# Attention and mixture of experts in one kernel: another hand-written order of transposes, routing steps and gating chain

## The chip, the cores and the metric

The kernel runs on one core of a Trainium2 chip. The metric is the device time of one execution in microseconds; before the change its median of three runs is 856.85 us (855.57 to 857.64). In the profile PE is the matrix engine (PEld its weight loads), DVE the vector engine, ACT the scalar engine, POOL GpSimd and SP the queue that issues most DMAs. The five engines run their own instruction queues, each in its order, and wait for each other by semaphores.

## The reference

Causal attention with a bias made from a cumulated sum, for 8 x 8 heads of 576 positions of 64 values, then a mixture of eight experts of which every token uses one:

```
cum = cumsum(max(s, 0))
scores = q @ k.T / 8 + min(-(cum[i] - cum[j]), 0)      # masked above the diagonal
attn_out = softmax(scores) @ v                         # per batch and head
x = attn_out with heads joined: (8 * 576, 512)
logits = x @ w_gate;  e = argmax(logits);  g = softmax(logits)[e]
out[token] = g * (max(x @ w1[e], 0) @ w2[e])           # e of that token
```

All in float32.

## The kernel before

The attention part works on 32 pairs of heads; four pairs are one batch element of 576 tokens. The rows of a pair are cut into four groups of 128 queries (0 to 3, with 128, 256, 384 and 512 keys, since later keys are masked) and a mixed group 4 that holds the last 64 rows of both heads (576 keys). The loop in `Attention.loop` goes over 32 x 5 units; `n` is the unit, `j = n % 5` its place in the pair, and `ORD` gives the groups in the order 3, 0, 2, 4, 1.

For each group of a pair there are these steps. `scores` (line 217) makes the score tile `s` in PSUM with four matmul terms per head: bias, and three products of high and low parts of q and k. `rowmax` (L257, DVE) reads `s`, adds the mask, and writes `z` and its row minimum `m`. `expo` (L271, ACT) writes the exponentials to `E`. `trans` turns `E` by half transposes on PE (L275) into a PSUM tile `t`, which DVE or ACT copies into `aT` (L297, L298: groups 0, 1, 4 on DVE, 2 and 3 on ACT). `av` (L308) multiplies a whole pair's `aT` with v, one pair later, and DVE copies the result into `xb` (L297). The next pair's q and k are split into high and low parts meanwhile, on ACT (L191, L197) and POOL (L194, L201).

PSUM tiles come from two pools of two buffers: `s` for scores and, while attention runs, for the routing steps; `t` for transposes and `av`. A score tile waits until DVE has read the tile two before it. `z` has four buffers.

After each fourth pair a batch element is routed, in eight steps that `begin` and `end` issue between the attention units, two a pair, both at j = 4: one ahead of the scores of group 1 and one behind the transposes there. Step 0 is the gating product (L351, with `w_gate`, copied to `LT` by ACT), step 1 turns `LT` (L275) and multiplies by the softmax denominators (`part`, L365). A chain of small DVE operations and one exponential follows (L373 to L394: logits, their maximum, the one-hot expert `oh`, the gate value). Step 2 ranks tokens within their expert by small matmuls (L401 to L404) and DVE operations (L410 to L416) and yields row numbers `dsi`. Steps 3 to 7 turn and scale 128 tokens each (L426, into `xr`). Once `dsi` is there, POOL scatters the rows to the experts' lists by indirect DMAs (L437), one per unit. The seventh batch element (b = 6) takes steps faster, since the first expert's load needs it; the eighth is routed after the loop, beside the first expert's work.

The order on PE, DVE and ACT is the order in which this code is written. The order on POOL and SP is made by a scheduler. `transposes` lag three units behind their scores (`LAG`), `expo` one unit; the list `STEPS` gives the order of the routing steps. `constants` (L817 to L849) fills small tables for routing with DVE and POOL.

## Time and profile before

| | |
|---|---|
| median of three runs | 856.85 us (855.57 to 857.64) |
| the profiled execution | 850.7 us, span 849.0 us, mean granted clock 0.980 |
| busy over the span | PE 784.9, PEld 624.1, DVE 483.7, ACT 426.2, POOL 209.3 us |
| attention | from the first scores at 9.28 us to the last value run at 379.8 us |

The profiled execution is 6.2 us below the median of the runs; differences worked out inside it are carried over to the median. In a row of the order of time stand the start in us, the duration, the engine, the line, the operation, output and inputs by the program's names, the shape, the count, and in brackets the idle time of the engine just before and what ended it. A matmul row with x2 or x12 joins as many instructions.

### The profile page before, as it was taken

The page shows a single profiled execution, that of the slowest core. Times are in us where ns is not written, and L with a number is a line of the kernel's source. Part 1 is how long each engine was busy: PE and PEld are TensorE (multiplying, and loading weights), DVE is VectorE, ACT ScalarE, POOL GpSimd, SP SyncE. Part 2 cuts the span into 40 slices and gives each one's busy share as a digit, 9 for nine tenths or more (in the row PEclk, how much of TensorE's full clock was granted, in tenths as well). Part 3 has the DMA queues.
Part 4 walks back from the last instruction along what each step waited for, and adds up shares of the span by engine and source line. Part 5 has one row for each costly group of instructions (what it writes and reads, how often), then busy time and mean ns, then how long its engine had stood idle before and what let it go on. Part 6 is the DMA issues. An engine that isn't in the chain of part 4 may idle for free.

```text
span 849.0 us, 17331 instructions
## 1 busy us (share of the span) xinstructions
PE 784.9 (92%) x6708; PEld 624.1 (74%) x6708; DVE 483.7 (57%) x1264; ACT 426.2 (50%) x1006; POOL 209.3 (25%) x309
## 2 busy tenths in 40 slices
PE   6899898998998999799989999999999999899994
PEld 4677766676767776566878878888888888788883
DVE  6777878787878777768516445353362263542511
ACT  5787777777777777663315233332251251422401
POOL 5333535363545444502010100001001001001010
PEclk8899999999999999899999999999999999999997
DMA  6373424243333332155955354351161062531110
GB/s 218 118 228 105 139 88 144 89 138 95 109 100 106 107 125 80 39 169 201 283 170 178 124 162 163 128 183 38 44 227 68 18 225 87 188 125 33 50 50 15
DMA packets 43901, 105.21 MB, mean 124 GB/s; under 512 B 3983, under 2 KB 3983, under 8 KB 43792
## 3 DMA queue, kind: packets, MB, share of 16 engines
q1 hardware_dynamic: 35408, 80.13, 29.6%
q0 software_dynamic: 5936, 18.92, 6.2%
q10 hardware_dynamic: 2448, 4.74, 1.6%
q8 instruction: 66, 1.08, 0.5%
q14 instruction: 43, 0.35, 0.1%
HBM read 75.91 MB, written 28.12 MB: 123 GB/s over the span
## 4 chain that ended last, share of the span: by engine, by line
issue 40%; PE 31%; DVE 11%; DMA 7%; ACT 3%; another core or an unknown queue 3%; POOL 3%; POOLq 1%; SPq 0%; DVEq 0%; ACTq 0%
PE s L217 12%; PE t L308 8%; DMA out_dram<-y,xr 6%; DVE z L257 5%; PE t L275 4%; PE ph L651 3%; PE py L673 3%; POOL out_dram L680 2%; ACT E L271 2%; PE s L351 1%; DMA raw<-in_w_dram 1%; DVE aT L297 1%; ACT q L191 1%; ACT kh L197 1%
## 5 line engine op out<-in xcount | busy, mean ns | idle before, releaser
L673 PE MATMUL py<-w2t,hT 128*128 128x512 f32 x768 | 181.6, 392 | 0.0
L651 PE MATMUL ph<-xT,w1t 128*128 128x512 f32 x768 | 178.4, 391 | 3.3 <-issue 2.4
L271 ACT ACTIVATE E<-z,m 128x512 f32<-128x512 f32 (+4 forms) x288 | 165.2, 577 | 22.4 <-DVE m L257 22.0
L257 DVE CUSTOM_DVE_ANT_0 z<-s,mask 128x512 f32<-128x512 f32 (+4 forms) x288 | 139.3, 517 | 53.9 <-PE s L217 18.8
L651 PEld LDWEIGHTS ph<-xT,w1t 128*128 128x128 f32 x768 | 143.3, 188 | 34.9 <-issue 4.9
L673 PEld LDWEIGHTS py<-w2t,hT 128*128 128x128 f32 x768 | 142.5, 188 | 28.9
L680 POOL DMA_INDIRECT out_dram<-y,xr x39 | 38.0, 975 | 397.3 <-DVE y L679 355.8
L217 PE MATMUL s<-cu,pick 64*128 64x512 f32 (+4 forms) x320 | 76.7, 397 | 26.9 <-DVE m L257 19.2
L308 PE MATMUL t<-aT,v 128*64 128x64 f32 (+4 forms) x1152 | 96.8, 322 | 3.2 <-DVE aT L297 3.2
L275 PEld LDWEIGHTS t<-ident,E 64*128 64x128 f32 x1600 | 72.6, 141 | 33.6 <-ACT E L271 21.9
L653 ACT ACTIVATE hT<-ph 128x512 fp32r<-128x512 f32 x64 | 38.3, 598 | 108.6 <-PE ph L651 108.1
L679 DVE TENSOR_SCALAR y<-py,xr 128x512 f32<-128x512 f32 x35 | 26.3, 751 | 114.1 <-PE py L673 114.1
L298 ACT COPY aT<-t 128x1024 f32<-128x1024 f32 x64 | 57.9, 905 | 62.5 <-PE t L275 62.5
L654 DVE SCALAR_TENSOR_TENSOR hT<-ph,hT 128x512 fp32r<-128x512 f32 x64 | 44.3, 692 | 73.1 <-ACT hT L653 72.9
L217 PE MATMUL s<-kh,q 64*128 64x384 f32 (+3 forms) x512 | 84.2, 327 | 0.0
L275 PE MATMUL t<-ident,E 64*128 64x64 f32 x1600 | 81.4, 228 | 2.9 <-DVE xb L297 1.7
L308 PEld LDWEIGHTS t<-aT,v 128*64 128x64 f32 x1152 | 51.9, 139 | 25.2 <-issue 15.5
L217 PEld LDWEIGHTS s<-cu,pick 64*128 64x128 f32 (+1 forms) x320 | 39.4, 194 | 40.8 <-DVE m L257 14.7
L568 ACT ACTIVATE xT<-t 128x512 fp32r<-128x512 f32 x32 | 18.4, 597 | 89.5 <-PE t L624 89.5
L297 DVE COPY aT<-t 128x256 f32<-128x256 f32 (+2 forms) x96 | 61.6, 642 | 0.7 <-PE t L275 0.6
L194 POOL TENSOR_TENSOR q<-qk,q 128x576 fp32r<-128x576 f32 x31 | 44.4, 1431 | 60.9 <-ACT q L191 60.8
L271 ACT ACTIVATION_READ_ACCUMULATOR E<-z,m 128x1 f32 x288 | 54.5, 189 | 0.0
(155 smaller groups left out, 1027.7 us busy)
## 6 DMA issues: line engine op xcount, KB each, us to landing
raw<-in_w_dram SPq DMA_DIRECT2D x32, 1024.0 KB, 5.5
qk<-in_qkv_dram SPq DMA_DIRECT2D x32, 576.0 KB, 3.8
v<-in_qkv_dram SPq DMA_DIRECT2D x32, 320.0 KB, 3.6
xr<-xs SPq DMA_DIRECT2D x8, 1028.0 KB, 5.6
xs<-blank ACTq DMA_DIRECT2D x9, 514.0 KB, 6.1
xs<-blank SPq DMA_DIRECT2D x8, 514.0 KB, 8.5
xr<-xs SPq DMA_DIRECT2D x8, 514.0 KB, 6.4
xs<-xr,dsi POOLq DMA_INDIRECT x40, 3.4
```

The lines of the kernel that those rows point to most:

```text
L194: e.tensor_tensor(out=d["q"][:, 1], in0=q, in1=d["q"][:, 0].bitcast(F32), op=ALU.subtract)
L217: self.nc.tensor.matmul(out, terms[n][0], terms[n][1], start=n == 0, stop=n == len(terms) - 1, skip_group_check=True)
L257: ins = nc.vector.tensor_tensor_reduce(out=cut(z[:, :w]), in0=x, in1=mask, scale=-0.125, scalar=3.0e38, op0=ALU.add, op1=ALU.min, accum_out=m,
L271: nc.scalar.activation(out, z[:, :w], AF.Exp, bias=m, scale=-1.0, accum_out=total)
L275: self.nc.tensor.transpose(out, src[r], self.K["ident"][r, r])
L297: return self.nc.vector.tensor_copy(o, i)
L298: return self.nc.scalar.copy(o, i)
L308: nc.tensor.matmul(ps[64 * h : 64 * h + 64, bank, lo - 512 * bank : hi - 512 * bank], v[:, kt, h], self.aT[p % 2][:, kt, h, lo:hi], start= ...
L651: nc.tensor.matmul(ps, w[:, a, d, c], x[:, b, d], start=n == 0, stop=n == 11)
L654: nc.vector.scalar_tensor_tensor(out=h[:, 1, f], in0=ps, scalar=0.0, in1=h[:, 0, f].bitcast(F32), op0=ALU.max, op1=ALU.subtract)
L673: self.nc.tensor.matmul(ps, hT[:, a, f, c], w[:, b, f % 4], start=f == 0 and i == 0, stop=f == 7 and i == 2)
L680: disjoint(self.tc, "out", self.nc.gpsimd.indirect_dma_start(out=self.out, out_offset=IndirectOffsetOnAxis(ap=row[:, DM + 1 : DM + 2].bitc ...
```

## The change

It reorders what the loop issues and alters no arithmetic. The table `TURNS` replaces the fixed lag: at j = 1 the transposes of groups 4 and 1 of the pair before, at j = 3 those of group 3, at j = 4 those of groups 0 and 2 of the same pair. `EXPS` does the same for the exponentials. The steps of a batch element come as 3, 0, 1, 4, 5, 6, 2, 7, so that the token step 3 stands first behind the value run and the gating product second; batch 6 takes 3, 0, 1, 2, 4, 5, 6, 7 with one extra step a pair at j = 1 (before: at j = 1 and j = 2). The gating chain yields once more, behind its exponential, and its halves run at j = 3 of two successive pairs (both at once for batch 6). `constants` is a generator now, and its three pieces run in the first three units instead of all in the seventh.

```
--- before.py
+++ after.py
@@ -33,7 +33,8 @@
 ORD = (3, 0, 2, 4, 1)
 MIX = 4
 NG = len(ORD)
-LAG = 3
+TURNS = {1: (4, 1), 3: (3,), 4: (0, 2)}
+EXPS = {1: (3,), 2: (0,), 3: (2, 4), 4: (1,)}
 FILL0, FSTEP, FILL_END = 9, 2, 28
 RUNP = NPAIR
 WARM = 24
@@ -41,7 +42,8 @@
 SPLIT_AT = (0, 1, 0, 1, 3, 2)
 EVAC = {0: "V", 1: "V", 2: "A", 3: "A", 4: "V"}
 AV_AT = 3
-STEPS = (0, 3, 1, 4, 2, 5, 6, 7)
+STEPS = (3, 0, 1, 4, 5, 6, 2, 7)
+HASTE = (3, 0, 1, 2, 4, 5, 6, 7)
 W_STEP = 2
 THIN_AT = (2, 2)
 X0 = (1, 2, 1)
@@ -315,7 +317,7 @@
         if x == 3:
             r = dict(b=b, xb=xb)
             self.scale(r)
-            self.rq += [(r, i) for i in (range(self.NROUTE) if b >= RUNP // 4 - 2 else STEPS)]
+            self.rq += [(r, i) for i in (STEPS, HASTE, range(self.NROUTE))[max(0, b - RUNP // 4 + 3)]]
         self.copy("V", xb[:, x, :S], ps.rearrange("p a c -> p (a c)")[:, :S])
         self.st.pop(p)
 
@@ -381,6 +383,7 @@
             nc.vector.tensor_reduce(out=mx, in_=L, op=ALU.max, axis=AX.X)
             nc.vector.tensor_tensor(out=dd, in0=L, in1=mx.unsqueeze(2).broadcast_to([P, 5, 8]), op=ALU.subtract)
             nc.scalar.activation(ex, dd, AF.Exp)
+            yield
             nc.vector.scalar_tensor_tensor(
                 out=sc, in0=dd, scalar=0.0, in1=K["w8"].unsqueeze(1).broadcast_to([P, 5, 8]),
                 op0=ALU.is_ge, op1=ALU.mult,
@@ -453,16 +456,19 @@
         self.load(1)
         self.load_v(1)
         self.rq, self.sq, self.chain = [], [], None
-        soon = lambda: self.rq and self.rq[0][0]["b"] == RUNP // 4 - 2
+        hasty = lambda: self.rq and self.rq[0][0]["b"] == RUNP // 4 - 2
+        todo = constants(self.nc, self.const, self.K, self.wg)
         for n in range(nu + NG - 1):
             j = n % NG
+            now = n < nu
             first = None
-            if n < nu:
+            due = self.sq.pop(0) if self.sq and n >= FILL_END else None
+            if now:
                 p, g = steps[n]
                 if j == 0 and p + 2 < RUNP:
                     self.load(p + 2)
                     self.load_v(p + 2)
-                if n >= FILL0 and n < FILL_END and (n - FILL0) % FSTEP == 0 and self.nfill <= E:
+                if n >= FILL0 and (n - FILL0) % FSTEP == 0 and self.nfill <= E:
                     self.fill(self.nfill)
                     self.nfill += 1
                 if j == 4:
@@ -475,29 +481,32 @@
                 self.rowmax(p, g)
                 if first:
                     self.end(first)
-                if n == 6:
-                    constants(self.nc, self.const, self.K, self.wg)
-            due = self.sq.pop(0) if self.sq and n >= FILL_END else None
-            if j != 4 and 0 < n <= nu:
-                self.expo(*steps[n - 1])
+                next(todo, None)
+            if now:
+                for x in EXPS.get(j, ()):
+                    self.expo(p, x)
             if j == AV_AT:
-                if n < nu:
-                    self.expo(p, g)
                 if self.chain:
                     next(self.chain, None)
-                    self.chain = None
+                    if self.chained == RUNP // 4 - 2:
+                        next(self.chain, None)
                 if n >= NG:
                     self.av(n // NG - 1)
-            if 0 <= n - LAG < nu:
-                self.trans(*steps[n - LAG])
-            if n < nu and (j == 4 or j in (1, 2) and soon()):
+            for x, g2 in enumerate(TURNS.get(j, ())):
+                q = n // NG - (j == 1)
+                if 0 <= q < RUNP:
+                    self.trans(q, g2)
+                if now and j == 4 and x == 0:
+                    self.end(self.begin())
+            if now and j == 1 and hasty():
                 self.end(self.begin())
-            if n < nu and p + 1 < RUNP:
+            if now and p + 1 < RUNP:
                 for x in range(6):
                     if SPLIT_AT[x] == j:
                         self.split(p + 1, x)
             if due:
                 self.scatter(*due)
+        assert self.nfill > E
         assert all(r["b"] == RUNP // 4 - 1 for r, *x in self.rq + self.sq)
         self.open = False
 
@@ -505,9 +514,6 @@
         if not self.rq:
             return None
         r, x = self.rq.pop(0)
-        if x == 2 and self.chain:
-            next(self.chain, None)
-            self.chain = None
         todo = self.route(r, x)
         next(todo)
         return r, x, todo
@@ -517,7 +523,7 @@
             r, x, todo = step
             next(todo, None)
             if x == 1:
-                self.chain = todo
+                self.chain, self.chained = todo, r["b"]
             r.setdefault("ready", [])
             if x > 2:
                 r["ready"].append((r, x - 3))
@@ -528,9 +534,8 @@
     def finish(self):
         while self.rq:
             self.end(self.begin())
-            if self.chain:
-                next(self.chain, None)
-                self.chain = None
+            while self.chain:
+                self.chain = self.chain if next(self.chain, 0) is None else None
         while self.sq:
             self.scatter(*self.sq.pop(0))
 
@@ -823,23 +828,25 @@
     ramp = cp.tile([P, 8], I32, name="ramp")
     K["w8"] = cp.tile([P, 8], F32, name="w8")
     nc.gpsimd.iota(ramp, pattern=[[-1, 8]], base=8, channel_multiplier=0)
-    nc.vector.tensor_copy(K["w8"], ramp)
     ramp2 = cp.tile([P, 8], I32, name="ramp2")
     K["base0"] = cp.tile([P, 8], F32, name="base0")
     K["base"] = cp.tile([P, 8], F32, name="base")
     K["first"] = cp.tile([P, 8], F32, name="first")
     nc.vector.memset(K["first"], float(P * NSTAT))
     nc.gpsimd.iota(ramp2, pattern=[[STRIDE, 8]], base=0, channel_multiplier=0)
-    nc.vector.tensor_copy(K["base0"], ramp2)
-    nc.vector.tensor_copy(K["base"], ramp2)
     one = cp.tile([P, P], F32, name="one")
     nc.vector.memset(one, 1.0)
     low = cp.tile([P, P], F32, name="low")
     nc.gpsimd.affine_select(
         out=low, in_=one, pattern=[[1, P]], compare_op=ALU.is_gt, fill=0.0, base=0, channel_multiplier=-1
     )
+    yield
+    nc.vector.tensor_copy(K["w8"], ramp)
+    nc.vector.tensor_copy(K["base0"], ramp2)
+    nc.vector.tensor_copy(K["base"], ramp2)
     K["both"] = cp.tile([P, HP], F32, name="both")
     nc.vector.tensor_tensor(out=K["both"], in0=K["ident"][:, :HP], in1=K["ident"][:, HP:], op=ALU.add)
+    yield
     K["before"] = cp.tile([P, P], BF16, name="before")
     K["ones"] = cp.tile([P, P], BF16, name="ones")
     K["ones64"] = cp.tile([P, P], BF16, name="ones64")
```

The line numbers below are those of each program: what is line 217, 275, 297, 351, 373 before, is 219, 277, 299, 353, 375 after. `E_107`, `E_104`, `E_106`, `E_108` and `E_105` are the exponentials of groups 3, 0, 2, 4 and 1.

First place: PE at the end of a pair that has the gating product, from the transposes of group 3 behind the value run to the first scores of the next pair. Before:

```order
L275 MATMUL t<-ident,E_107 128x64 x16
L351 MATMUL s<-xb_197,wg 32x288 x8
L217 MATMUL s<-cu,pick 128x256 x2
L217 MATMUL s<-kh,q 128x256 x2
L217 MATMUL s<-kl,q 128x256 x2
L217 MATMUL s<-kh,q 128x256 x2
L275 MATMUL t<-ident,E_104 128x64 x4
L275 MATMUL s<-ident,xb_197 128x64 x8
L217 MATMUL s<-cu,pick 128x512 x2
```

And after:

```order
L277 MATMUL t<-ident,E_107 128x64 x16
L277 MATMUL s<-ident,xb_197 128x64 x8
L219 MATMUL s<-cu,pick 128x256 x2
L219 MATMUL s<-kh,q 128x256 x2
L219 MATMUL s<-kl,q 128x256 x2
L219 MATMUL s<-kh,q 128x256 x2
L277 MATMUL t<-ident,E_104 128x64 x4
L353 MATMUL s<-xb_197,wg 32x288 x8
L277 MATMUL t<-ident,E_106 128x64 x12
L219 MATMUL s<-cu,pick 128x512 x2
```

The gating product (`xb,wg`) and the eight token transposes have changed places, and the twelve transposes of group 2 now stand ahead of the 512-wide scores instead of behind them. In the other pairs the two routing steps are others, and the transposes of group 2 stand in the same new place.

Second place: PE in the middle of a pair, from the last scores of group 0 to the first of group 4. Before:

```order
L217 MATMUL s<-kh,q 128x128 x2
L275 MATMUL t<-ident,E_108 128x64 x10
L217 MATMUL s<-cu,pick 128x384 x2
L217 MATMUL s<-kh,q 128x384 x2
L217 MATMUL s<-kl,q 128x384 x2
L217 MATMUL s<-kh,q 128x384 x2
L275 MATMUL t<-ident,E_105 128x64 x8
L217 MATMUL s<-cu,pick 128x288
```

And after:

```order
L219 MATMUL s<-kh,q 128x128 x2
L277 MATMUL t<-ident,E_108 128x64 x10
L277 MATMUL t<-ident,E_105 128x64 x8
L219 MATMUL s<-cu,pick 128x384 x2
L219 MATMUL s<-kh,q 128x384 x2
L219 MATMUL s<-kl,q 128x384 x2
L219 MATMUL s<-kh,q 128x384 x2
L219 MATMUL s<-cu,pick 128x288
```

The eight transposes of group 1 have moved ahead of the 384-wide scores; behind these the scores of group 4 follow at once.

Third place: DVE in the third pair of a batch element's routing, from the start of the gating chain to the copy of the value product. Before, the whole chain:

```order
L373 TENSOR_TENSOR both<-part 128x160
L375 TENSOR_REDUCE L<-both 128x40
L381 TENSOR_REDUCE mx<-L 128x5
L382 TENSOR_TENSOR dd<-L,mx 128x40
L384 SCALAR_TENSOR_TENSOR sc<-dd,w_410 128x40
L389 TENSOR_REDUCE m_1455<-sc 128x5
L390 TENSOR_TENSOR oh<-sc,m_1455 128x40
L392 TENSOR_REDUCE sm<-ex 128x5
L393 TENSOR_SCALAR sm<-sm 128x5
L394 RECIPROCAL xr<-sm 128x5
L297 COPY xb_204<-t 128x576
```

After, in the third pair:

```order
L375 TENSOR_TENSOR both<-part 128x160
L377 TENSOR_REDUCE L<-both 128x40
L383 TENSOR_REDUCE mx<-L 128x5
L384 TENSOR_TENSOR dd<-L,mx 128x40
L299 COPY xb_204<-t 128x576
```

and in the fourth pair, where nothing of the chain stood before:

```order
L387 SCALAR_TENSOR_TENSOR sc<-dd,w_247 128x40
L392 TENSOR_REDUCE m_1652<-sc 128x5
L393 TENSOR_TENSOR oh<-sc,m_1652 128x40
L395 TENSOR_REDUCE sm<-ex 128x5
L396 TENSOR_SCALAR sm<-sm 128x5
L397 RECIPROCAL xr<-sm 128x5
L299 COPY xb_204<-t 128x576
```

The chain is cut behind the difference `dd`; its second half stands one pair later, and the ranking step, which needs `oh`, with it.

More of the change, by code (lines that the diff above doesn't have):

```diff
@@ L455, in loop @@
         self.rq, self.sq, self.chain = [], [], None
-        soon = lambda: self.rq and self.rq[0][0]["b"] == RUNP // 4 - 2
+        hasty = lambda: self.rq and self.rq[0][0]["b"] == RUNP // 4 - 2
+        todo = constants(self.nc, self.const, self.K, self.wg)
         for n in range(nu + NG - 1):
             j = n % NG
+            now = n < nu
             first = None
-            if n < nu:
+            due = self.sq.pop(0) if self.sq and n >= FILL_END else None
+            if now:
                 p, g = steps[n]
@@ L477, in loop @@
                     self.end(first)
-                if n == 6:
-                    constants(self.nc, self.const, self.K, self.wg)
-            due = self.sq.pop(0) if self.sq and n >= FILL_END else None
-            if j != 4 and 0 < n <= nu:
-                self.expo(*steps[n - 1])
+                next(todo, None)
+            if now:
+                for x in EXPS.get(j, ()):
+                    self.expo(p, x)
             if j == AV_AT:
-                if n < nu:
-                    self.expo(p, g)
                 if self.chain:
                     next(self.chain, None)
-                    self.chain = None
+                    if self.chained == RUNP // 4 - 2:
+                        next(self.chain, None)
                 if n >= NG:
                     self.av(n // NG - 1)
-            if 0 <= n - LAG < nu:
-                self.trans(*steps[n - LAG])
-            if n < nu and (j == 4 or j in (1, 2) and soon()):
+            for x, g2 in enumerate(TURNS.get(j, ())):
+                q = n // NG - (j == 1)
+                if 0 <= q < RUNP:
+                    self.trans(q, g2)
+                if now and j == 4 and x == 0:
+                    self.end(self.begin())
+            if now and j == 1 and hasty():
                 self.end(self.begin())
-            if n < nu and p + 1 < RUNP:
+            if now and p + 1 < RUNP:
                 for x in range(6):
@@ L507, in begin @@
         r, x = self.rq.pop(0)
-        if x == 2 and self.chain:
-            next(self.chain, None)
-            self.chain = None
         todo = self.route(r, x)
@@ L840, in constants @@
     )
+    yield
+    nc.vector.tensor_copy(K["w8"], ramp)
+    nc.vector.tensor_copy(K["base0"], ramp2)
+    nc.vector.tensor_copy(K["base"], ramp2)
     K["both"] = cp.tile([P, HP], F32, name="both")
     nc.vector.tensor_tensor(out=K["both"], in0=K["ident"][:, :HP], in1=K["ident"][:, HP:], op=ALU.add)
+    yield
     K["before"] = cp.tile([P, P], BF16, name="before")
```

22 lines of the change are left out of this document (11 added, 11 removed).

## The prediction

> **What bounds the kernel now.** I read the table of stages first, then the order of time on PE inside one attention pair, then who ends PE's waits there. Names: S3, S0, S2, S4, S1 are the score matmuls of a pair in the order of issue; M, X and T with the same number are that group's row minimum on DVE, exponentials on ACT and transposes on PE; xb is the copy of the value product; A and B are the two routing steps of a pair.
>
> The page's group of first score matmuls and the stage of one full turn of four pairs (columns: stretch, its length, busy time of PE, PE's weight loads, DVE, ACT, POOL, granted clock, DMA):
>
> ```profile
> L217 PE MATMUL s<-cu,pick 64*128 64x512 f32 (+4 forms) x320 | 76.7, 397 | 26.9 <-DVE m L257 19.2
> 112.67:157.41 44.74, 40.79 (x584) 31.32 (x582) 34.57 (x117) 33.88 (x90) 21.04 (x30) 1.00 0.35 111
> ```
>
> Four pairs take 44.74 us, PE is busy for 40.79 of them, DVE for 34.57, ACT for 33.88. PE is nearest to its bound but idle for 3.95 us a turn, and most of the idle time before scores ends with a row minimum. The clock is 1.00. Where the idle time lies, one pair with A and B both token steps (PE):
>
> ```profile
> 133.54 0.49 PE L217 MATMUL s<-cu,pick 64*128 64x512 f32 x2 [0.47 <-DVE base L416]
> ...
> 134.55 0.56 PE L275 MATMUL t<-ident,E 64*128 64x64 f32 x12
> 134.89 0.33 PE L217 MATMUL s<-cu,pick 64*128 64x128 f32 x2
> ...
> 135.37 0.52 PE L275 MATMUL t<-ident,E 64*128 64x64 f32 x10
> 136.14 0.44 PE L217 MATMUL s<-cu,pick 64*128 64x384 f32 x2 [0.25 <-DVE m L257]
> ...
> 136.95 0.41 PE L275 MATMUL t<-ident,E 64*128 64x64 f32 x8
> 137.29 0.40 PE L217 MATMUL s<-cu,pick 128*128 128x288 f32 x1
> ...
> 138.54 3.06 PE L308 MATMUL t<-aT,v 128*64 128x64 f32 x36
> 141.54 0.71 PE L275 MATMUL t<-ident,E 64*128 64x64 f32 x16
> ...
> 143.29 0.46 PE L275 MATMUL s<-ident,xb 64*128 64x64 f32 x8
> 144.10 0.50 PE L217 MATMUL s<-cu,pick 64*128 64x512 f32 x2 [0.36 <-DVE m L257]
> ```
>
> and DVE in the same pair (M3's second half, xb, the token scaling of A, M1's second half):
>
> ```profile
> 135.39 0.69 DVE L257 CUSTOM_DVE_ANT_0 z<-s,mask 128x512 f32<-128x512 f32 x1
> ...
> 141.66 0.76 DVE L297 COPY xb<-t 128x576 f32<-128x576 f32 x1 [1.27 <-PE t L308]
> ...
> 142.54 0.69 DVE L426 TENSOR_TENSOR xr<-s,rr 128x512 f32<-128x512 f32 x1
> ...
> 143.53 0.42 DVE L257 CUSTOM_DVE_ANT_0 z<-s,mask 128x256 f32<-128x256 f32 x1
> ```
>
> The pair has two fixed distances. S2 needs the bank of S3: M3 ends at 136.08, S2 starts at 136.14, 2.60 us after S3. The next S3 needs the bank of S1: M1 ends at 143.95, S3 starts at 144.10, 2.56 us after T3. Between them PE never waits: S2 0.81, T1 0.34, S4 1.25, the value run 3.00. So pair = 2.60 + 5.40 + 2.56 = 10.56. T2 stands in the first distance, T1 in the middle, and at both ends PE idles.
>
> **The change, part by part.** *The two transposes.* T1 moves ahead of S2 into the first distance, T2 out of it and ahead of the next S3. The first distance then holds T1's 0.34 in place of T2's 0.34 (134.55 to 134.89) and stays 2.60. The middle loses T1: 5.06. T2 lands in the 0.81 us from B's start to S3, of which B's eight transposes need 0.34, like T1's eight, and T2 0.34; the second distance stays 2.56, set by xb, the token scaling and M1 on DVE, which all hang on the value run. Each routed pair loses 0.34; T1's and T2's copies keep their engines, and ACT's queue keeps its order. Pairs with no routing step have no such idle time: T2 adds there what T1 saves, nothing. Bounds: 0 (T2 held by T3's copy on ACT) to 0.34 + 0.36, the whole wait of S3. I take 0.34.
>
> *The gating product second.* With it first, and waiting for xb, the pair of the product goes so; the last row is the same product later, unhindered:
>
> ```profile
> 152.10 0.71 PE L275 MATMUL t<-ident,E 64*128 64x64 f32 x16
> 152.75 1.56 PE L351 MATMUL s<-xb,wg 128*32 128x288 f32 x16
> ...
> 156.06 0.50 PE L217 MATMUL s<-cu,pick 64*128 64x512 f32 x2 [0.55 <-DVE m L257]
> ...
> 385.88 1.18 PE L351 MATMUL t<-xb,wg 128*32 128x288 f32 x16
> ```
>
> T3 to S3 is 3.96, since S1 and M1 stand behind the 1.5 us of product. After the change the token step is first; its last transposes wait for xb (ready 0.88 after T3), so its scaling on DVE ends near 1.9 after T3, where above it ended at 1.69. Then B, the product, 1.1 (385.88 to its end at 387.06, less the drain), then T2 0.34: 3.4. M1 is done by 2.8 and no longer counts. Saved 0.55 a turn; bounds 0 and 3.96 - 2.56 = 1.4.
>
> *The gating chain in halves.* Before, all of it stands between M4 and xb in one pair; rows of PE's T3, the chain's first and xb behind its last, and the ranking's first and last on DVE:
>
> ```profile
> 129.97 0.71 PE L275 MATMUL t<-ident,E 64*128 64x64 f32 x16
> ```
> ```profile
> 128.73 0.32 DVE L373 TENSOR_TENSOR both<-part 128x160 f32<-128x160 f32 x1
> ...
> 131.15 0.72 DVE L297 COPY xb<-t 128x576 f32<-128x576 f32 x1
> ...
> 132.47 0.20 DVE L410 TENSOR_TENSOR t<-s,base 128x40 f32<-128x40 f32 x1
> ...
> 133.24 0.15 DVE L416 TENSOR_TENSOR base<-base,s 128x8 f32<-128x8 f32 x1
> ```
>
> The chain is 2.4 us, xb starts 1.18 after T3 (0.12 in the pair above), and S3 of 133.54 waits for L416: T3 to S3 is 3.57. A half of 1.2 us fits: DVE idles 1.27 ahead of xb above, under the value run; without that cover each half would cost its 1.2. That pair becomes an ordinary one, 2.56: saves 1.01. But the ranking moves into the fourth pair, whose B now stands behind M1 and L416 too. There xb is on time, the ranking matmuls go ahead of S1, then M1 and 0.9 us of ranking. Bounds: 2.56 (hidden) to 3.57; I take 3.3, nearer the top, since L416 still ends last: costs 0.75. Left: 0.26. The batch's five scatters follow the ranking, all into the next product pair; POOL is busy for 21.04 of 44.74 and I count them at nothing, or, if they held up its subtractions for the next pair, at their lateness.
>
> A turn saves 4 x 0.34 + 0.55 + 0.26 = 2.17. Pairs 4 to 27 are six turns: **13.0 us**.
>
> *The seventh batch's haste.* Its S3 rows of pairs 29, 30 and 31, and the ranking between:
>
> ```profile
> 336.77 0.50 PE L217 MATMUL s<-cu,pick 64*128 64x512 f32 x2 [0.48 <-DVE m L257]
> ...
> 343.50 0.19 PE L401 MATMUL s<-oh,before 128*128 128x40 bf16 x1 [4.38 <-DVE oh L390]
> ```
> ```profile
> 353.81 0.50 PE L217 MATMUL s<-cu,pick 64*128 64x512 f32 x2 [0.35 <-DVE m L257]
> ```
> ```profile
> 364.76 0.47 PE L217 MATMUL s<-cu,pick 64*128 64x512 f32 x2
> ```
>
> Pair 29 takes 17.04 and pair 30 10.95: PE stands 4.38 us at the ranking, with S2 and the value run queued behind it. Now one extra step goes ahead of S2 in each, not two, and the chain runs under the value run. An extra step needs M3's bank (2.60) and holds one that S4 wants until DVE, behind M0 and two copies, has read it (about 4.95): S4 starts 1.55 later than the 3.41 above. Pair 29: 10.22 + 1.55 + 0.75 (ranking) + 0.2 (the whole chain slightly longer than the value run) = 12.7; pair 30: 10.22 + 1.55 = 11.8. 27.99 becomes 24.5: 3.5, and pair 28, a product pair, saves 0.34 + 0.55: **4.4 us**, bounds 2 and 6. The last scatter moves from pair 30 into pair 31, and expert 0's load waits for it. I count that at nothing, since most of pair 31 and a value run still follow; past that cover each us late is one us lost.
>
> *The constants* move from one block in pair 1 to three pieces in pair 0 (DVE; M3 of pairs 1, 2, 3, and the block):
>
> ```profile
> 11.86 1.46 DVE L158 TENSOR_SCALAR aT<-aT 128x384 f32<-128x384 f32 x1
> ...
> 23.98 0.69 DVE L257 CUSTOM_DVE_ANT_0 z<-s,mask 128x512 f32<-128x512 f32 x1 [0.90 <-PE s L217]
> ...
> 26.17 0.99 DVE L826 CAST w<-ramp 128x8 f32<-128x8 int32 x1
> ...
> 27.07 0.16 DVE L834 CAST base<-ramp 128x8 f32<-128x8 int32 x1
> ...
> 27.29 1.30 DVE L842 TENSOR_TENSOR both<-ident 128x64 f32<-128x64 f32 x1
> 29.49 0.23 DVE L846 CAST before<-low 128x128 bf16<-128x128 f32 x1 [0.91 <-POOL low L838]
> ```
> ```profile
> 37.69 0.69 DVE L257 CUSTOM_DVE_ANT_0 z<-s,mask 128x512 f32<-128x512 f32 x1
> ```
> ```profile
> 46.94 0.69 DVE L257 CUSTOM_DVE_ANT_0 z<-s,mask 128x512 f32<-128x512 f32 x1
> ```
>
> Pair 1 takes 13.71 where pair 2 takes 9.25: 4.46 saved. In pair 0 the pieces stand on the chain of bias tables that PE waits for. Of two like casts one took 0.99 and one 0.16. The 4.46 less 0.8 for the casts, 1.1 for `both` (estimated at 0.2 undisturbed) and the 0.91 of waiting leave 1.7 for the pieces; with casts and `both` as dear as here, and L158 held up by another 1.3, they cost 4.9. Net between +2.8 and -0.4; nearer the top, because only the first piece falls where L158 was long: **2.0 us**. [...]
>
> Pair 31 adds 0.3. Sum: 13.0 + 4.4 + 2.0 + 0.3 = 19.7. The profiled execution took 850.7 (span 849.0), so it would take 831.0; the median of the runs is 856.85, 6.2 above it, and gives **837**.
>
> **The rivals.**
> *T2 held.* T2 needs the bank that T3's copy frees; if that is late, S3 moves by T2's 0.34 in 27 routed pairs and 9.2 us of the gain go: 846. ACT in the quoted pair (T3's copy, then T2's):
>
> ```profile
> 142.29 1.02 ACT L298 COPY aT<-t 128x1024 f32<-128x1024 f32 x1 [1.00 <-PE t L275]
> ...
> 145.71 0.80 ACT L298 COPY aT<-t 128x768 f32<-128x768 f32 x1 [0.96 <-PE t L275]
> ```
>
> For: T3's copy ends at 143.31 and T2 would start near 143.6, 0.3 in hand. Against: ACT waits for PE, not PE for it.
> *PE full.* All 3.95 us idle a turn go, 23.7 in place of 13.0: 826. Against: M1 still hangs on xb.
> *No gain.* The waits move to M1 and M4, the turn stays 44.74, the haste gives its low 2, the startup loses 0.4: 855.3. Against: the middle run of PE shows no wait for DVE at all.
> *Slower: T1 blocks PE.* T1 needs the bank freed by T2's copy, and S2, S4 and the value run queue behind T1. S1's exponentials start behind M1, 143.95, and would end some 0.6 after S3, T2's copy 0.8 later, at 1.4; T1's turn comes at 1.83, and S2 could wait until 2.60 anyway, so it is free until 2.26. It costs beyond that, and beats the gain of about 0.73 a routed pair once the copy ends past 3.0; at 3.4 it costs 0.4 x 27 = 11: 868. For: one copy in a queue with the exponentials of S1 and, in product pairs, another copy ahead. Against: ACT is busy for 33.88 of 44.74.
>
> **How the numbers follow.** Forecast 0.53, own range 831 to 842 (startup 2.8 to -0.4, haste 2 to 6, the fourth pair's 0 to 1.01); T2 held 0.21; PE full 0.12; no gain 0.06; slower 0.08. Range 828 to 848: it holds the forecast, T2 held and the nearer part of PE full. About 0.2% (1.7 us) is what a measurement here can tell: faster 0.86, same 0.06, slower 0.08.
>
> **What would show it.** S2 still 2.60 after S3, its wait ended by M3; 5.06 from S2 to T3; no idle time ahead of S3 in product pairs; pairs of a turn near 11.1, 10.2, 10.2 and 11.0; a turn of 42.6; no 4.38 us gap; pair 1 near 9.3. Wrong if S3 waits on ACT, T1 waits on ACT, or pair 0 grows by over 4.

## The result, and the profile after

The changed kernel takes 842.84 us (median of four runs, 841.56 to 844.66) where the kernel before took 856.21 (855.45 to 857.64): ratio 0.9844, 95% interval 0.9818 to 0.9869, 13.4 us less. The forecast was 837, its range 828 to 848. The first of the four runs was profiled: 841.56 us, span 839.8. Against the profiled execution of before (span 849.0) that is 9.2 us, where the forecast had 19.7, so the two profiles show less gain than the medians, and the question is which terms fell short.

The page of the changed kernel, its first line and the groups of first score matmuls and of transposes:

```profile
span 839.8 us, 17309 instructions
L219 PE MATMUL s<-cu,pick 64*128 64x512 f32 (+4 forms) x320 | 72.4, 373 | 24.3 <-DVE m L259 16.1
L277 PE MATMUL t<-ident,E 64*128 64x64 f32 x1600 | 74.9, 227 | 3.8 <-ACT aT L300 3.6
```

PE's idle time ahead of the scores has gone from 26.9 only to 24.3 us, and 3.6 us of idle time that ACT ends now stand ahead of transposes (0.9 us before). The stages up to pair 31, cut at the S3 of pairs 4, 28 and 31 (columns as in the prediction's table of stages). Before:

```profile
0.00:54.84 54.84, 44.12 (x463) 31.36 (x464) 37.10 (x107) 36.47 (x93) 23.11 (x63) 0.88 0.54 177
54.84:324.77 269.93, 245.93 (x3468) 189.14 (x3465) 207.76 (x700) 204.18 (x543) 125.41 (x180) 0.99 0.37 118
324.77:364.76 39.99, 32.81 (x453) 25.44 (x453) 28.74 (x92) 24.79 (x68) 17.92 (x24) 0.91 0.15 50
```

After:

```profile
0.00:53.56 53.56, 41.77 (x474) 29.47 (x476) 35.01 (x112) 37.43 (x94) 23.72 (x64) 0.94 0.56 187
53.56:319.21 265.65, 238.32 (x3470) 179.94 (x3465) 202.08 (x696) 203.91 (x545) 121.02 (x174) 1.00 0.36 116
319.21:355.91 36.70, 30.92 (x452) 23.18 (x452) 27.32 (x96) 25.43 (x66) 19.95 (x26) 1.00 0.18 64
```

The startup gives 1.3 us (forecast 2.0), the six turns 4.3 (13.0), the haste 3.3 (4.4). The turns are where the gain is missing. An ordinary pair does what the prediction said (PE; S3, S2 with its wait for M3, T3, the next S3):

```profile
163.88 0.51 PE L219 MATMUL s<-cu,pick 64*128 64x512 f32 x2
...
166.60 0.44 PE L219 MATMUL s<-cu,pick 64*128 64x384 f32 x2 [0.53 <-DVE m L259]
...
171.65 0.71 PE L277 MATMUL t<-ident,E 64*128 64x64 f32 x16
...
174.21 0.49 PE L219 MATMUL s<-cu,pick 64*128 64x512 f32 x2
```

S2 to T3 is 5.05 (5.06 forecast), T3 to S3 2.56 in the third pair of the turn (2.56 forecast). The product pair does not. PE there, then DVE, ACT and POOL:

```profile
148.83 0.71 PE L277 MATMUL t<-ident,E 64*128 64x64 f32 x16
149.38 0.66 PE L277 MATMUL s<-ident,xb 64*128 64x64 f32 x8
...
152.00 1.18 PE L353 MATMUL s<-xb,wg 128*32 128x288 f32 x16 [1.32 <-DVE xr L429]
...
153.51 0.48 PE L219 MATMUL s<-cu,pick 64*128 64x512 f32 x2
```
```profile
148.94 0.76 DVE L299 COPY xb<-t 128x576 f32<-128x576 f32 x1
151.26 0.69 DVE L429 TENSOR_TENSOR xr<-s,rr 128x512 f32<-128x512 f32 x1 [1.55 <-PE t L277]
```
```profile
150.50 1.01 ACT L300 COPY aT<-t 128x1024 f32<-128x1024 f32 x1 [1.77 <-PE s L219]
```
```profile
148.46 1.01 POOL L440 DMA_INDIRECT xs<-xr,dsi  x1 [0.28 <-POOL qd L207]
149.77 0.93 POOL L440 DMA_INDIRECT xs<-xr,dsi  x1 [0.30 <-DVE xb L299]
```

T3 to S3 is 4.68, forecast 3.4. The token transposes of A end at 150.04, DVE is free from 149.70, yet the token scaling starts at 151.26, 1.2 us later. Its row names PE. ACT is late too: T3's transposes end at 149.54, and ACT's copy of them starts at 150.50. So both engines wait for word from PE. The semaphore events of the trace show it: PE's updates for these two groups of transposes come at 150.48 and 151.23, 0.94 and 1.20 us behind the ends of the matmuls, and DVE starts 0.03 us after the second. (The profile models the ends of matmuls, so this does not tell whether the matmuls or only their signals were late; PE's own rows go on without a gap to 150.68.) I call this a hold. The product, second behind the scaling, waits 1.32. Two scatters run on POOL at that time. In the product pair of the first batch, when there is nothing to scatter yet, the scaling starts 0.04 us after the transposes and the pair takes 11.24; in the next 0.64 us are lost (11.89), and in the five behind it 1.18 to 1.37 (12.4 to 12.6).

In the pairs without routing, PE is held at T2 (PE, then ACT):

```profile
51.34 0.71 PE L277 MATMUL t<-ident,E 64*128 64x64 f32 x16
...
53.16 0.59 PE L277 MATMUL t<-ident,E 64*128 64x64 f32 x12 [0.46 <-ACT aT L300]
53.56 0.48 PE L219 MATMUL s<-cu,pick 64*128 64x512 f32 x2
```
```profile
52.10 1.01 ACT L300 COPY aT<-t 128x1024 f32<-128x1024 f32 x1 [1.52 <-PE t L277]
```

T3's copy ends at 53.11, T2 starts at 53.16. These pairs went from 9.25 to 9.95 us.

### The profile page after: what moved, and what is told of

It is laid out like the page before. It is cut to its first block, busy times and chain, and to the rows that moved or that the text cites. A ratio compares the mean times of both kernels' runs of the same rounds, so it can differ in the third digit from the quotient of the medians.

```text
span 839.8 us, 17309 instructions
## 1 busy us (share of the span) xinstructions
PE 772.8 (92%) x6708; PEld 610.2 (73%) x6708; DVE 473.7 (56%) x1264; ACT 426.6 (51%) x1006; POOL 208.8 (25%) x309
## 4 chain that ended last, share of the span: by engine, by line
PE 39%; issue 38%; DVE 7%; DMA 7%; another core or an unknown queue 3%; POOL 2%; ACT 2%; POOLq 1%; SPq 0%; DVEq 0%; ACTq 0%
PE s L219 14%; PE t L310 11%; PE t L277 6%; DMA out_dram<-y,xr 6%; DVE z L259 4%; PE ph L656 3%; PE py L678 3%; POOL out_dram L685 2%; PE s L277 2%; DVE xr L429 1%; PE s L353 1%; DMA raw<-in_w_dram 1%; ACT aT L300 1%; ACT q L193 0%
## 5 line engine op out<-in xcount | busy, mean ns | idle before, releaser
L259 DVE CUSTOM_DVE_ANT_0 z<-s,mask 128x512 f32<-128x512 f32 (+4 forms) x288 | 134.6, 517 | 39.7 <-PE s L219 19.1
L219 PE MATMUL s<-cu,pick 64*128 64x512 f32 (+4 forms) x320 | 72.4, 373 | 24.3 <-DVE m L259 16.1
L310 PE MATMUL t<-aT,v 128*64 128x64 f32 (+4 forms) x1152 | 94.6, 318 | 0.0
L277 PEld LDWEIGHTS t<-ident,E 64*128 64x128 f32 x1600 | 62.4, 140 | 33.4 <-ACT E L273 22.8
L277 PE MATMUL t<-ident,E 64*128 64x64 f32 x1600 | 74.9, 227 | 3.8 <-ACT aT L300 3.6
L219 PE MATMUL s<-kh,q 64*128 64x384 f32 (+3 forms) x512 | 77.9, 320 | 0.0
L219 PEld LDWEIGHTS s<-cu,pick 64*128 64x128 f32 (+1 forms) x320 | 37.7, 190 | 42.1 <-DVE m L259 19.6
L310 PEld LDWEIGHTS t<-aT,v 128*64 128x64 f32 x1152 | 50.3, 137 | 21.3 <-issue 15.8
L299 DVE COPY aT<-t 128x256 f32<-128x256 f32 (+2 forms) x96 | 59.3, 642 | 4.1 <-PE t L277 3.5
```

Source lines behind the costliest of these rows:

```text
L219: self.nc.tensor.matmul(out, terms[n][0], terms[n][1], start=n == 0, stop=n == len(terms) - 1, skip_group_check=True)
L259: ins = nc.vector.tensor_tensor_reduce(out=cut(z[:, :w]), in0=x, in1=mask, scale=-0.125, scalar=3.0e38, op0=ALU.add, op1=ALU.min, accum_out=m,
L277: self.nc.tensor.transpose(out, src[r], self.K["ident"][r, r])
L299: return self.nc.vector.tensor_copy(o, i)
L310: nc.tensor.matmul(ps[64 * h : 64 * h + 64, bank, lo - 512 * bank : hi - 512 * bank], v[:, kt, h], self.aT[p % 2][:, kt, h, lo:hi], start= ...
```

## The experiments

The first four kernels ran on one chip (kernel before: 857.03 us), the next four on a second (852.45), the last four on a third (853.75). Ratios are to the kernel before on the same chip. Lengths of pairs are counted here from one M3 to the next, unless S3 is named.

### What holds the token scaling

The last two scatters of a batch behind the scaling:

```
+            if step == 3:
+                self.gate = ins.ins.name          # the token scaling
...
+        if k > 2 and r["b"] < RUNP // 4 - 2:
+            after(self.tc, ins, [self.gate])       # in scatter
-            due = self.sq.pop(0) if self.sq and n >= FILL_END else None
+            due = self.sq.pop(0) if self.sq and n >= FILL_END and j < 3 else None
```

> The changed kernel, with the last two of a batch's five scatters held back until the token scaling of A in the product pair has been issued (a wait for it, and two units later in the program); nothing else. Theory 1 (the scatters hold the token scaling): in the changed kernel the scaling of A in the product pair starts 1.17 to 1.41 us after its transposes end in pairs 12, 16, 20, 24 and 28 and 0.68 us in pair 8, where scatters run on POOL just ahead, and 0.04 us in pair 4, where there are none. Here it starts 0.04 to 0.1 us after them everywhere, the product pairs go from 12.4 (11.88) to 11.2 us, and the time falls by 1.2 x 5 + 0.65 = 6.7 us, from 842.8 to about 836. Theory 2 (its own waits hold it, five semaphores of the scatters two batches ago): the lag stays at 1.2 us and the time at 842.8.

Measured: 841.81 us, ratio 0.9815 (0.9791 to 0.9839). The lag is gone, 0.04 to 0.10 us in all product pairs, but these fell only to some 11.75 (one 12.11). DVE in one of them, then POOL:

```profile
194.08 0.69 DVE L429 TENSOR_TENSOR xr<-s,rr 128x512 f32<-128x512 f32 x1 [0.37 <-PE s L277]
...
198.17 0.69 DVE L259 CUSTOM_DVE_ANT_0 z<-s,mask 128x512 f32<-128x512 f32 x1 [2.35 <-PE s L219]
```
```profile
195.16 1.04 POOL L442 DMA_INDIRECT xs<-xr,dsi  x1 [0.16 <-DVE m L259]
196.50 0.92 POOL L442 DMA_INDIRECT xs<-xr,dsi  x1 [0.30 <-issue]
```

The hold has moved with the scatters: M3 of the next pair now starts 0.75 us behind the end of the last of them, though S3 ended at 197.51; PE's update for S3 comes 0.53 us late. Pair 30 became longer too (13.34 for 11.79); 3.41 us of it, from 345.83, ran at a granted clock of 0.50, which hides part of the gain.

The buffer's own waits passed earlier:

```
+        nc.vector.memset(r["xr"][:, :, DM], 0.0)   # first line of the buffer's use, ahead of xb
```

> The changed kernel, with a small write to the new xr buffer (its gate column, 128 x 5) on DVE ahead of the value run's copy, so that DVE passes the five semaphores of the buffer's earlier scatters there and not at the token scaling. Theory 1 (the scatters of this very pair hold the scaling): the lag of 1.2 us stays, product pairs stay 12.4, time 842.8 (plus 0.1). Theory 2 (the five waits hold it): the lag goes in pairs 12, 16, 20, 24 and 28 (pair 8 keeps its 0.68), and the time falls by 6 us to about 837.

Measured: 841.26 us, ratio 0.9834 (0.9810 to 0.9859). The scaling stays late, 1.16 to 1.21 us behind its transposes in five pairs:

```profile
147.74 0.76 DVE L299 COPY xb<-t 128x576 f32<-128x576 f32 x1
149.99 0.69 DVE L430 TENSOR_TENSOR xr<-s,rr 128x512 f32<-128x512 f32 x1 [1.49 <-PE t L277]
```

So not its waits but the scatters. In the pair that had lost 0.64 the scaling starts 0.04 us behind them here, with the same scatters; the hold is sensitive to timing. (Pair 29 took 13.99 us here, with 3.41 us at clock 0.50.) The third piece of evidence is the changed kernel again on the third chip:

> The changed kernel once more. In its first profile the token scaling of the product pair was held 1.2 us in five of seven pairs; in the run with the constants in one block, which has the same five scatters at the same times (POOL's last two start 1.61 and 0.30 us before the scaling could start, as in the first profile), it was not held at all. Theory 1 (the hold depends on the chip, since that run was on another one): on the chip of this call all seven product pairs are of one kind, either 12.4 or 11.25 us, and 12.4 only if it is the first chip. Theory 2 (it depends on the kernel's code, such as where the constants stand): 12.4 again. Without the hold the time is about 6 us lower against the kernel before than the 0.984 measured first: 0.978.

Measured: 838.33 us, ratio 0.982 (0.9794 to 0.9847); product pairs 11.23 to 11.30 throughout. DVE, ACT and POOL at the same place:

```profile
148.62 0.76 DVE L299 COPY xb<-t 128x576 f32<-128x576 f32 x1 [0.40 <-PE t L310]
149.75 0.69 DVE L429 TENSOR_TENSOR xr<-s,rr 128x512 f32<-128x512 f32 x1 [0.38 <-PE s L277]
```
```profile
149.25 1.01 ACT L300 COPY aT<-t 128x1024 f32<-128x1024 f32 x1 [1.52 <-PE t L277]
```
```profile
148.16 1.01 POOL L440 DMA_INDIRECT xs<-xr,dsi  x1 [0.28 <-POOL qd L207]
149.47 0.93 POOL L440 DMA_INDIRECT xs<-xr,dsi  x1 [0.30 <-DVE xb L299]
```

The scatters start 1.59 and 0.28 us before the scaling, where in the first profile they stood 1.61 and 0.30 before the moment at which it could have started. The same program, at offsets that agree to some 0.03 us, is held in the first measurement and not here; ACT's copy starts 0.04 us after T3. PE's semaphore updates sort the traces in the same way. Up to the end of attention, 37 to 51 of them come more than 0.3 us late in the first measurement and in three runs on the first chip (late scatters, early waits, T2 back); the fourth run there has late ones too. On the other two chips, eight traces, not one does, and not one in the profile of before (0.01 to 0.04 us throughout). So it goes with the chip, or with the occasion, since each chip served for one set of runs. The stages of this run:

```profile
0.00:53.90 53.90, 42.80 (x474) 29.94 (x476) 34.93 (x112) 37.44 (x94) 23.69 (x64) 0.91 0.55 185
53.90:313.91 260.01, 238.24 (x3469) 179.80 (x3465) 203.84 (x696) 203.30 (x545) 121.09 (x174) 1.00 0.37 118
313.91:349.46 35.55, 30.95 (x452) 23.20 (x452) 27.53 (x96) 25.36 (x66) 19.98 (x26) 1.00 0.19 66
```

Without the hold the turns give 9.9 us against the profile of before, and the haste 4.4.

### The chain whole again

```
-STEPS = (3, 0, 1, 4, 5, 6, 2, 7)
+STEPS = (3, 0, 1, 4, 2, 5, 6, 7)
...
                 if self.chain:
                     next(self.chain, None)
-                    if self.chained == RUNP // 4 - 2:
-                        next(self.chain, None)
+                    next(self.chain, None)
+                    self.chain = None
```

> The changed kernel with the gating chain whole again in the third pair and the ranking there (steps 3, 0, 1, 4, 2, 5, 6, 7); transposes, product second and haste as changed. The scatters then follow in the fourth pair and leave the product pair. Theory 1 (scatters hold the token scaling in the product pair): third pair from 10.3 to about 11.3, fourth from 11.3 to about 10.4, product pair from 12.4 to 11.2: about 1.1 us a turn less over five turns, 5 to 6 us, about 837. Theory 2 (waits of the buffer hold it): product pair stays 12.4, third and fourth trade places, time 842 to 843.5.

Measured: 836.55 us, ratio 0.9755 (0.9734 to 0.9777), 6.3 us less than the first measurement of the changed kernel. Product pairs 11.23 to 11.29, third pairs 11.1, fourth 10.3 (one 10.8). The scatters now run in the fourth pair. PE's updates are late there too, by up to 2.4 us, but only in the pair of 10.8 does it cost anything. On the third chip, where nothing is held anyway:

> The run with the whole chain in the third pair once more, beside the changed kernel. Where the scatters hold the scaling in the product pairs, it is 5 to 6 us faster than the changed kernel, as measured on the first chip (836.6 to 842.8). Where they do not, third and fourth pair only trade places (11.1 + 10.32 in place of 10.33 + 11.31): 0.2 us a turn, 1 us in all, no difference that can be told.

Measured: 836.59 us, ratio 0.9812 (0.9788 to 0.9836), against 838.33 for the changed kernel; the intervals overlap. By one turn each, 43.23 us (changed) and 43.05 (whole):

```profile
140.77:184.00 43.23, 39.68 (x578) 29.96 (x578) 34.01 (x117) 33.80 (x91) 21.04 (x30) 1.00 0.35 115
```
```profile
140.02:183.07 43.05, 39.76 (x580) 30.00 (x579) 33.55 (x117) 33.79 (x92) 21.02 (x31) 1.00 0.36 115
```

The halves themselves are worth nothing (0.2 us a turn the wrong way); where signals come late they cost 6 us by moving the scatters.

### T2 back behind the next S3

```
-TURNS = {1: (4, 1), 3: (3,), 4: (0, 2)}
+TURNS = {0: (2,), 1: (4, 1), 3: (3,), 4: (0,)}
...
-                q = n // NG - (j == 1)
+                q = n // NG - (j < 2)
```

> The changed kernel with only T2 put back behind S3 of the next pair (T1 stays ahead of S2). Theory 1 (in pairs without routing T2 is held by T3's copy on ACT and pushes S3): pairs 2 and 3 go from 9.95 back to about 9.3, three pairs, 2.0 us less; in the ordinary routed pairs the distance T3 to S3 stays 2.56 to 2.64, set by M1; in product pairs it loses T2's 0.34. What it costs: T1 needs the bank of T2's copy, which ended 2.4 us after S3 in the kernel before, so S2 would come at about 2.85 after S3 in place of 2.70: 0.15 x 28 = 4 us. Sum: 842.8 - 2.0 - 2.0 + 4 = about 843. Theory 2 (the slow pairs without routing come from T1 ahead of S2): pairs 2 and 3 stay at 9.95. If T1 is held longer than that (past 3.0 after S3), the time is over 848.

Measured: 853.2 us, ratio 0.9954 (0.9940 to 0.9968), 10 us over the expected 843. What was expected came: pairs without routing at 8.9 to 9.0, ordinary pairs unchanged at 10.4, 10.3 and 11.3, the first product pair at 10.96, T1 hardly held (S2 comes 2.73 us after S3, not the feared 2.85). But POOL's scheduler put all five scatters in one row, and the product pairs took 13.4 to 15.8. DVE and POOL in one:

```profile
145.93 1.42 DVE L299 COPY aT<-t 128x640 f32<-128x640 f32 x2 [2.96 <-remote]
```
```profile
138.88 1.05 POOL L440 DMA_INDIRECT xs<-xr,dsi  x1 [1.55 <-DVE base L419]
...
144.07 0.92 POOL L440 DMA_INDIRECT xs<-xr,dsi  x1 [0.30 <-issue]
```

T4's transposes had ended at 141.14; their copy waits until 0.94 us after the last scatter's end, and the value run behind it. The row's "remote" is an update that the view can't assign; by its semaphore it is PE's, and it comes at 145.91, 4.8 us late. This is the largest hold seen. In the three longest product pairs (15.5 to 15.8) it is followed by 3.41 us at a granted clock of 0.50, here from 146.54, so not all of their length is the hold itself.

With the chain whole, so that the scatters stand elsewhere:

> The run with the whole chain in the third pair (836.55 us), with T2 also put back behind S3 of the next pair. With T2 back alone (853.2 us) the pairs without routing fell from 9.95 to 9.0, ordinary routed pairs stayed at 10.4 and 10.3, the one product pair without scatters fell from 11.23 to 10.96, and the product pairs with scatters rose to 13.5 to 15.7, since all five scatters then ran in one row and held DVE. Theory 1 (scatters hold DVE; T2 is held by T3's copy): here the scatters stand in the fourth pair, so no product pair rises: 3 x 0.95 + 7 x 0.27 = 4.7 us less, about 832. Theory 2 (T2 behind S3 by itself lengthens the product pairs, through T1 or the copies on ACT): product pairs of 13 us and more again, over 845.

> The whole chain with T2 behind S3, once more, beside the run without T2's move: by the pairs of its first profile (8.95 in place of 9.95 in three, 10.9 in place of 11.25 in seven) 5 us less than the whole chain alone, 0.994 of it. Rival: its profile had a granted clock of 0.96 in the attention stretches where the whole chain had 1.00; if a fuller PE is throttled more, half of the 5 us or all of it goes.

Measured: 835.56 us on the second chip (ratio 0.9791, 0.9766 to 0.9817) and 836.52 on the third (0.9795, 0.9767 to 0.9823; the whole chain alone has 836.59 there). No product pair rises as with T2 back alone. They take 10.9 us at best and up to 0.9 more: in the longest, pair 16, DVE's scaling of the softmax sums (L335) ran beside a POOL subtraction on both chips, its second part took 1.46 us on the third, and the value copy behind it was late. The startup gets 4.0 us shorter (the S3 of pair 4 at 49.54 in place of 53.53), and yet the gain is gone: in the profiled executions, from the second turn on the fourth pairs take 11.5 in place of 10.2 us, S3 to S3, and S2 in them comes 3.9 us after S3. PE's clock, in stretches of 3.41 us around the end of a third pair:

```profile
118.72:122.13 3.41, 3.41 (x47) 1.93 (x47) 3.09 (x13) 3.21 (x13) 1.97 (x3) 1.00 0.32 68
122.13:125.54 3.41, 2.40 (x45) 1.89 (x43) 3.07 (x16) 2.10 (x5) 0.79 (x3) 1.00 0.57 202
125.54:128.95 3.41, 3.41 (x37) 3.14 (x37) 1.94 (x6) 1.02 (x2) 2.80 (x3) 0.50 0.42 158
```

For 3.41 us the granted clock is 0.50, once in each of five turns, and each time the stretch of 3.41 us ahead of it is one of the five emptiest of the turns (PE busy 2.4 of 3.41 us or a little more). The rival, that a fuller PE is slowed down, does not fit that: with T2 behind S3, the ranking's waits at the end of the third pair have no transposes left to fill them. But the busy share alone does not decide it. Later in the same run a stretch that is emptier still is followed by full clock:

```profile
340.57:343.98 3.41, 2.34 (x34) 1.88 (x31) 3.41 (x12) 3.41 (x11) 2.74 (x3) 1.00 0.28 101
343.98:347.39 3.41, 3.41 (x42) 2.00 (x40) 1.00 (x4) 2.19 (x8) 1.79 (x4) 1.00 0.20 77
```

The five executions of this kernel on the second chip differ in the same way: from 842.54 us at a mean granted clock of 0.971 (the profiled one) their times fall in the order of the clock to 831.48 us at 0.986, and the last is the 832 that was expected. In the whole chain without T2's move back the clock stays at 1.00 over the turns; the stretch at the same place there:

```profile
127.10:130.51 3.41, 2.60 (x45) 2.30 (x46) 2.95 (x12) 2.86 (x7) 1.28 (x3) 1.00 0.34 96
```

### The old transposes, the product first, the constants in one block

All transposes where the kernel before has them, the rest as in the whole chain:

```
+TURNS = {0: (2,), 1: (4,), 2: (1,), 3: (3,), 4: (0,)}
...
+                q = n // NG - (j < 3)
```

> The run with the whole chain in the third pair, with all transposes where the kernel before has them: T2 behind S3 of the next pair, T1 behind S2. Only the product's place, the haste and the constants are then as changed. The prediction's theory (T1 ahead of S2 is worth 0.34 us in each pair with routing, since the middle of the pair loses it and the first distance stays): against the run with T2 alone put back (expected 832), T1 adds 0.25 to 0.34 us in 28 pairs, 7 to 9.5 us: 839 to 841; pairs without routing back at 9.25. Rival (T1's place is worth nothing): 832.

Measured: 839.18 us, ratio 0.9854 (0.9832 to 0.9877). Against the whole chain with T2 put back on the same chip (835.56) 3.6 us more; that kernel lost up to 6 us to its clock, so the two don't compare by their times. By pairs at full clock, S2 to T3 is 5.29 here and 5.03 there: T1's place is worth some 0.25 in the routed pairs. The product pair with neither T1 nor T2 moved:

```profile
146.77 0.72 PE L277 MATMUL t<-ident,E 64*128 64x64 f32 x16
...
149.87 0.50 PE L219 MATMUL s<-cu,pick 64*128 64x512 f32 x2
```

T3 to S3 is 3.10, in the changed kernel 3.50: T2 ahead of S3 costs 0.40 there.

The product first again:

```
-STEPS = (3, 0, 1, 4, 2, 5, 6, 7)
+STEPS = (0, 3, 1, 4, 2, 5, 6, 7)
```

> The run with the whole chain in the third pair (836.55 us), with the gating product first behind the value run again and the token step second (steps 0, 3, 1, 4, 2, 5, 6, 7). The prediction's theory: T3 to S3 in the product pair goes from 3.4 to 3.96, 0.55 us more (0.4 by the 11.25 us that a product pair without scatters took against 11.96 before, less T1's 0.3): 7 pairs, 3 to 4 us, about 840. Rival (the order of product and token step is worth nothing): 836.5.

Measured: 839.68 us, ratio 0.9863 (0.9835 to 0.9892).

```profile
148.82 0.71 PE L277 MATMUL t<-ident,E 64*128 64x64 f32 x16
...
152.66 0.49 PE L219 MATMUL s<-cu,pick 64*128 64x512 f32 x2 [0.18 <-DVE m L259]
```

T3 to S3 is 3.84 against 3.50 with the product second. Over the six turns the difference is some 0.3 us, in one pair 0.6. S3 waits for M1 again.

The constants in one block in the changed kernel:

```
-                next(todo, None)
+                if n == 6:
+                    list(todo)
```

> The changed kernel with the constants in one block in the seventh unit again. By the two profiles pair 0 then loses 1.06 us (14.40 to 13.34) and pair 1 gains 3.75 (9.97 to 13.7): 2.7 us more, 845.5. If the pair 0 of the changed kernel is longer for another reason (exponentials and transposes in other places), it stays at 14.4 and the cost is 3.7 us, 846.5.

Measured: 839.83 us, ratio 0.9856 (0.9831 to 0.9882), on the second chip, where the changed kernel itself was not run. The S3 of pair 4 stands at 55.95 us, in the run of the changed kernel on the third chip at 53.90: the pieces are worth 2.05 us by these two runs. Other runs with the same startup have that S3 at 53.3 to 55.0 us, so the worth lies between 1.0 and 2.6. The expected 2.7 to 3.7 was too high, since pair 0 did not get shorter (15.45 against 14.40 and 14.75). This run's product pairs were not held either (11.23 to 11.30), with its last scatters 1.61 and 0.30 us ahead; that was the hint at the chip.

### A shorter chain

To see whether the third pair of the whole chain (T3 to S3 3.46) is long because the chain does not fit under the value run, its last three operations at the end of the pair, in the kernel that also has T2 behind S3:

```
+            r["oh"] = oh
+            yield                                   # sum, addend, reciprocal: at the end of j = 4
             sm = rt.tile([P, 5], F32, name="sm")
```

> The whole chain with T2 behind S3, with the last three operations of the gating chain (sum of the exponentials, its addend, the reciprocal: needed by the scatters only) taken out of the stretch ahead of the value run's copy and put at the end of the pair, where DVE idles 0.56 us ahead of the next M3. The theory that the third pair (11.1 us) is 0.7 longer than the second because the chain of 2.4 us does not fit into DVE's 1.83 us under the value run: the three operations are about 0.6 us, so the third pair falls to about 10.5, 0.55 x 6 = 3.3 us less, and the haste is unchanged. Rival (the third pair is set by the ranking behind M1, not by the chain): no change.

Measured: 838.56 us, ratio 0.9803 (0.9778 to 0.9829), against 836.52 with the chain whole; the intervals overlap. T3 to S3 is 3.57 where it was 3.46, so the rival holds:

```profile
79.97 0.75 DVE L299 COPY xb<-t 128x576 f32<-128x576 f32 x1
81.49 0.42 DVE L259 CUSTOM_DVE_ANT_0 z<-s,mask 128x256 f32<-128x256 f32 x1 [0.77 <-PE t L277]
```

The value copy starts 0.3 us after T3 in place of 0.8, and DVE then idles 0.77 us ahead of M1: it waits for PE, where the ranking's matmuls stand ahead of S1.

## Why the prediction was right, and where it was not

The time lay in the range, just outside the forecast's own (831 to 842), and nearer to the time of the rival "T2 held" (846) than to 837, though not for that rival's reason: in the routed pairs T2 was not held. That the range covers the time is luck as far as the hold goes, which nothing in it priced. Otherwise the mechanism is the predicted one and the sum was too large, by 4.3 us where nothing is held (853.75 to 838.33 is 15.4, forecast 19.7), and by 6.3 in the first measurement. That measurement's record doesn't name its chip; its kernel before, 856.2, and its held pairs are like the first chip's. The profile of before that the sum was built on, 850.7, has no late update, and its time is nearer to that of the other two chips; whether it comes from the same chip is open. By its terms:

| term | forecast us | measured |
|---|---|---|
| T1 out of the middle, per routed pair | 0.34 | 0.24 (5.29 to 5.05) |
| T1 and T2 in pairs without routing | 0 | cost 0.7 together in three pairs |
| product second: T3 to S3 | 3.96 to 3.4 | 3.83 to 4.01 (once 4.80) to 3.50; 4.68 where held |
| third pair without the chain: T3 to S3 | 3.57 to 2.56 | 3.57 to 2.56 |
| fourth pair with the ranking: T3 to S3 | 2.56 to 3.3 | 2.57 to 3.57 |
| scatters in the product pair | 0 | 0; 5.6 in the turns and 1.2 in pair 28 where PE's signals come late |
| haste, pairs 28 to 30 | 4.4 | 4.4; 3.3 where held |
| constants | 2.0 | 2.05, by other runs 1.0 to 2.6 |

**The pair.** The three distances were read from one pair, the one with two token steps, and it was not typical. The next pair of the same profile shows it:

```profile
144.10 0.50 PE L217 MATMUL s<-cu,pick 64*128 64x512 f32 x2 [0.36 <-DVE m L257]
...
146.81 0.45 PE L217 MATMUL s<-cu,pick 64*128 64x384 f32 x2 [0.36 <-DVE m L257]
```

S3 to S2 is 2.71, not 2.60, and the middle 5.29, not 5.40; the sum is the same. After the change all pairs have 2.70 and 5.05. In the quoted pair the middle did lose 0.35, but its first distance grew by 0.1; in the others the first distance stayed, set by M3 as predicted, and the middle lost 0.24. That is 0.1 x 24, 2.4 us of the missing gain.

**T2 hidden.** True in the ordinary routed pairs, where M1 sets S3, and the rival's condition (T2's bank freed too late) did not arise there. The step that failed is "T2 adds there what T1 saves, nothing", for the pairs without routing: there T3's copy holds T2, and the pairs lost 0.7 us each (9.00 us with T2 put back, 9.95 without), which is most of why the startup gave 0.9 to 1.3 us although the constants gave about the predicted 2.0. In the product pair T2's place costs 0.40, which the sum of 3.4 had included.

**The fourth pair.** The value taken, 3.3, was near the top of its bounds; it is the top, 3.57, the same as the third pair had before. Chain and ranking simply changed places, so the chain in halves saved nothing where 0.26 a turn was forecast.

**The scatters.** This is the step that failed in the first measurement. The prediction saw that five scatters would move into the product pair, and priced only what they could do to POOL's own subtractions. Beside them PE's signals came late, and the scaling of A hung on one of these. There was no row in the profile of before that showed such a hold, nor a late update, but there was a bound to be had: the scatters and the scaling of A would be neighbours in time, and a scatter takes about 1 us on POOL (0.92 to 1.19 in that profile); had that been put in as a loss of 1 us in each product pair, the low end of the gain would have been 6 us lower.

**The haste and the constants** came as priced: pair 29 took 12.6 and pair 30 11.7 us (12.7 and 11.8 forecast), and the 4.38 us gap at the ranking is gone. The low end of the constants counts a further 1.3 us on the bias operation (L158, now L160); no run shows that term. The operation took 0.80 us in place of 1.46, since the first piece moved its start but not its end (13.34 and 13.32 us).

Of the 9.9 us that the turns gave without the hold, some 1.8 belong to none of these terms: two of before's pairs are 0.9 us longer than their kind. In pair 16, T3 to S3 is 4.80, since DVE's scaling of the softmax sums took 1.37 us beside a POOL subtraction (0.17 to 0.58 in the other batches) and the value copy came late. In pair 27, PE ran for 3.41 us at half clock:

```profile
313.68:317.09 3.41, 3.41 (x40) 3.19 (x38) 2.12 (x9) 1.39 (x3) 2.67 (x3) 0.50 0.40 154
```

## What to carry to other kernels

Read a fixed distance from several pairs, not from one, before a sum is built on it. When a reordering brings GpSimd's indirect DMAs next to the operation that a chain hangs on, price a hold of that operation, about 1 us for each such place (here 0.64 to 1.37 us at the scaling on one chip, none on two others), and move the DMAs rather than the chain. The version to keep is the changed kernel with the chain left whole: its scatters fall in a pair where a late signal is mostly not on the path, and its granted clock stayed at 1.00 over the turns. (With T2 put back as well it measures the same.) When an engine waits for a matmul that has ended by its row, see whether a second engine waits too: here ACT's copy started 0.96 us behind its transposes beside DVE's scaling, 1.2 us behind its own, which spoke for late signals and not for a hold of DVE alone. And idle time on PE may not be free to concentrate: here, with T2 put back, the granted clock fell to 0.50 for 3.41 us in each of five turns once transposes had left a stretch with waits.
